# A searched order of all steps in place of planned dates, and other buffers for the last results

## The chip, the cores and the metric

One Trainium2 chip, one of its cores. The metric is the time of the whole program on that core in microseconds (us), median of several runs. One further execution was recorded by the hardware profiler; its rows are quoted below.

## The reference

Two stages. First, linear attention over 8 batches x 8 heads of 576 positions with 64 features:

```python
def phi(x):                                   # q and k: 8 x 8 x 576 x 64, w_phi: 64 x 128
    proj = np.einsum('bhsd,df->bhsf', x, w_phi)
    proj = proj - np.max(np.abs(proj), axis=-1, keepdims=True)
    return np.concatenate([np.exp(proj), np.exp(-proj)], axis=-1)
q_p, k_p = (phi(q), phi(k))
kv = np.einsum('bhsf,bhsd->bhfd', k_p, v)
z = np.sum(k_p, axis=2)
num = np.einsum('bhsf,bhfd->bhsd', q_p, kv)
den = np.einsum('bhsf,bhf->bhs', q_p, z)[..., None] + 1e-06
attn = num / den
```

Then a layer on the 4608 x 512 result x: `h = x @ w_in` (512 x 2048), `g = h * cos(h)`, `out = g @ w_out` (2048 x 512). All in float32.

## The kernel before

**Work.** A *unit* u is a pair of heads; there are 32. The 4608 rows of x are nine *chunks* c of 512 rows, and the inner width of 2048 is 16 blocks of 128 (ft). A *tile* is one chunk with one block; there are 144. Each becomes a float32 product out of three reduced ones (xh, xl, gh, gl and the two parts of w are high and low parts).

**Steps.** Each piece of work is a `Step` with an engine, a planned cost, the steps it depends on, and the buffers that it takes and uses. There are 2885 of them. A unit's steps on TensorE (PE) are q_mm (q projected, two steps), k_mm and k_end (k projected), k_sub (the row maximum subtracted, units 0 to 7), kv_mm, z_mm (the denominator) and n_mm (the numerator). ScalarE (ACT) copies q, computes the exponentials and copies kv; VectorE (DVE) takes maxima and divides; GpSimd (POOL) subtracts; SyncE (SP) issues all loads and stores. A tile's steps are mm1 (h, twelve matmuls, PE), copy and cosine and high (ACT), reduce, times and low (DVE), then mm2 (twelve matmuls into four banks, one for each 128 rows of the chunk). The first mm2 of a visit to a chunk is cut into four steps called `one`, one for each bank. When a visit ends, four `out_copy` steps (two on ACT, two on DVE) bring the banks into buffers o, and four `out_store` steps on SP send them off.

**Shapes of matmuls.** mm1, mm2, k_end and k_sub use the array as 128 x 128; q_mm and k_mm as two halves of 64 rows; kv_mm and n_mm as two halves of 64 columns; z_mm as four quarters of 32 columns.

**Order.** Chunks 0 to 2 are visited several times while the weights are converted; chunks 3 to 8 once each, with half of the weights loaded again per visit. Attention units stand between the tiles until all 32 are through. Which step comes when is decided in `plan()`: it keeps the time at which each engine, buffer and PSUM bank would be free by the planned costs, and takes of the steps that could start next the one with the earliest `due`. The dates come from a pace (`U_PE`, `T_PE`, `SPAN`, `SHIFT`, ...) and from two tables of corrections, `EARLIER` for each kind of step and `LATER` for each unit, block and visit. Each engine runs its steps in the order of the plan, and an instruction waits on the chip for the others by semaphores.

**Buffers.** Each name in `rings` has a fixed number of buffers, used in turn: o has 2, eq (exponentials of q) 3, gh and gl 3 each. There are 8 PSUM banks.

Of the kernel before, what the change touches and what calls it, by code (L numbers as in the profile page):

```python
# [17 lines left out]
P = 128  # L18
# [7 lines left out]
def phi_attention_then_cos_ffn(ctx: ExitStack, tc: tile.TileContext, qT, kT, vS, vT, w_phi, w_in, w_out, out):  # L26
# [36 lines left out]
    in_ring = {}  # L63
# [5 lines left out]
    class Step:  # L69
        def __init__(self, eng, cost, fn, deps=(), take=(), use=(), due=0.0, lat=None, table=None, port=False, kind=""):  # L70
# [4 lines left out]
            self.kind, self.due = kind, due + EARLIER.get(kind, 0.0)  # L75
# [3 lines left out]
            self.start, self.group = None, ""  # L79

            ring = tuple(b.ring for b in self.take if b.ring != "bank")
            self.after = [in_ring[ring]] if ring in in_ring else []
            if ring:
                in_ring[ring] = self
# [24 lines left out]
    LATER = {  # L109
# [7 lines left out]
    }  # L117
    TURN = dict(ACT=131.0, PE=97.0)
    SLACK = dict(PE=0.05, ACT=0.05, DVE=0.05, POOL=0.05, SP=0.05)
    LATENCY = dict(PE=0.35, ACT=0.25, DVE=0.2, POOL=0.25, SP=2.2)  # L120

    def plan():
        free = dict.fromkeys(LATENCY, 0.0)
        free["port"] = 0.0
        taken = {r: [] for r in rings}
        owner = [None] * 8
        todo = {e: [] for e in LATENCY}
        users = {}
        missing = {}
        for x in steps:  # L130
            missing[x] = len(x.deps) + len(x.after)
            for d in x.deps + x.after:
                users.setdefault(d, []).append(x)
        for x in steps:
            if not missing[x]:
                todo[x.eng].append(x)
        order = []
        table = dict(ACT=None, PE=None)

        def ready(x):  # L140
            t = max(free[x.eng], free["port"]) if x.port else free[x.eng]
            for d in x.deps:
                t = max(t, d.start + d.cost + d.lat)
            for b in x.take:
                if b.ring == "bank":
                    continue
                old = taken[b.ring]
                want = sum(1 for o in x.take[:x.take.index(b)] if o.ring == b.ring)
                k = len(old) + want - rings[b.ring]
                if k >= 0:  # L150
                    for v in old[k].users:
                        if v.start is None:
                            return None
                        t = max(t, v.start + v.cost + v.lat)
            n = sum(1 for b in x.take if b.ring == "bank")
            if n:
                open_ = [c[0] for c in empty()]
                if len(open_) < n:
                    return None
                t = max(t, open_[n - 1])  # L160
                if x.take[0].kind == "a" and x.due > FFN_DUE or x.take[-1].kind == "a" and x.due > FFN_DUE:
                    held = sorted(end_of(b) for b in owner if b is not None and b.kind == "a")
                    if len(held) + n > A_BANKS:
                        t = max(t, held[len(held) + n - A_BANKS - 1])
                        if t > 1e8:
                            return None
            return t

        def end_of(b):
            return max(1e9 if v.start is None else v.start + v.cost + v.lat for v in b.users)  # L170

        def empty():

            found = []
            for i, b in enumerate(owner):
                if b is None:
                    found.append((0.0, i))
                elif all(v.start is not None for v in b.users):
                    found.append((max(v.start + v.cost + v.lat for v in b.users), i))
            return sorted(found)  # L180

        while len(order) < len(steps):
            best = None
            for e, xs_ in todo.items():
                can = [(ready(x), x) for x in xs_]
                can = [c for c in can if c[0] is not None]
                if not can:
                    continue
                t = min(c[0] for c in can)
                x = min((c for c in can if c[0] <= t + SLACK[e]),  # L190
                        key=lambda c: c[1].due + (TURN[c[1].eng] if c[1].table not in (None, table.get(c[1].eng)) else 0.0))
                if best is None or x[0] < best[0]:
                    best = x
            assert best is not None, [(e, len(v)) for e, v in todo.items()]
            t, x = best
            x.start = t
            c = x.cost
            if x.table not in (None, table.get(x.eng)):
                c += SWITCH[x.table]
                table[x.eng] = x.table  # L200
                x.cost = c
            free[x.eng] = t + c
            if x.port:
                free["port"] = t + c
            spare = empty()
            for b in x.take:
                if b.ring == "bank":
                    b.slot = spare.pop(0)[1]
                    owner[b.slot] = b
                else:  # L210
                    taken[b.ring].append(b)
            todo[x.eng].remove(x)
            order.append(x)
            for y in users.get(x, []):
                missing[y] -= 1
                if not missing[y]:
                    todo[y.eng].append(y)
# [714 lines left out]
```

## Time and profile before

| | us |
|---|---|
| median of 3 runs | 1108.19 |
| range of the runs | 1107.01 to 1110.52 |
| the profiled execution's own time | 1109.67 |
| its span, first to last instruction | 1107.7 |
| TensorE busy | 1090.7 |
| VectorE busy | 743.3 |
| ScalarE busy | 724.2 |

The span is what the rows of the trace divide up; the execution's own time has 2.0 us more around it. An engine's busy time is a union over the span. Matmuls overlap in the profile, so the time of a matmul step is best read from its start to the start of the next one. The mean granted clock of TensorE over the span is 0.996 of full speed.

### The profile page before, as it was taken

How to read it: one execution, taken by the hardware profiler on the slowest of the kernel's cores; microseconds unless marked ns; L12 is line 12 of the kernel's file. 1: busy time of each engine (PE TensorE's matmuls, PEld its weight loads, DVE VectorE, ACT ScalarE, POOL GpSimd, SP SyncE). 2: the span in 40 equal slices, each digit the busy share in tenths (PEclk: the TensorE clock that was granted, in tenths of full speed). 3: DMA queues.
4: the chain of work that ended last, by engine and by line, in shares of the span. 5: the costliest groups of instructions: out<-in, count | busy, mean ns of one | idle time of the engine just before them, and what ended most of it. 6: DMA issues, size and time to landing. Idle time of an engine off the chain costs nothing.

```text
span 1107.7 us, 19579 instructions
## 1 busy us (share of the span) xinstructions
PE 1090.7 (98%) x7664; PEld 826.0 (75%) x7664; DVE 743.3 (67%) x1298; ACT 724.2 (65%) x1386; POOL 128.3 (12%) x91
## 2 busy tenths in 40 slices
PE   8999999999999999999999999999999999999998
PEld 5556566778887877778767787778676888888886
DVE  6889999988899775684587636784665334433432
ACT  6688889967775777664567746796577445444443
POOL 2655122000000210110031101120210000000000
PEclk9999999999999999999999999999999999999999
DMA  7466454556666433535243542444313611430531
GB/s 218 148 190 208 154 159 147 185 209 218 248 211 231 137 100 107 160 106 192 72 147 83 185 163 59 154 149 173 100 28 124 221 73 58 170 134 3 192 147 38
DMA packets 92604, 160.72 MB, mean 145 GB/s; under 512 B 43744, under 2 KB 52064, under 8 KB 84320
## 3 DMA queue, kind: packets, MB, share of 16 engines
q1 hardware_dynamic: 92512, 159.48, 42.8%
q8 instruction: 60, 0.98, 0.4%
q14 instruction: 32, 0.26, 0.1%
HBM read 117.51 MB, written 41.94 MB: 144 GB/s over the span
## 4 chain that ended last, share of the span: by engine, by line
PE 84%; DVE 5%; ACT 2%; DMA 0%; issue 0%; DVEq 0%
PE bank L783 34%; PE bank L817 12%; PE bank L818 11%; PE bank L819 11%; PE bank L676 4%; PE bank L627 4%; PE bank L439 2%; PE bank L666 2%; PE bank L477 2%; PE bank L633 1%; PE bank L552 0%; DMA sums<-o 0%; DVE o L862 0%; ACT L798 0%; DVE m_u__1175 L458 0%
## 5 line engine op out<-in xcount | busy, mean ns | idle before, releaser
L798 ACT ACT_TABLE_LOAD x22 | 28.2, 1283 | 0.4
L468 POOL TENSOR_TENSOR pq_u__3813<-pq_u__3813,bq_u__4068 128x576 f32<-128x576 f32 x2 | 3.6, 1802 | 173.8 <-DVE bq_u__4068 L464 173.8
L862 DVE COPY o<-bank 128x512 f32<-128x512 f32 x18 | 12.3, 683 | 8.3 <-PE bank L819 5.6
L860 ACT ACTIVATE o<-bank 128x512 f32<-128x512 f32 x18 | 10.7, 596 | 8.9 <-PE bank L819 5.7
L587 ACT ACT_TABLE_LOAD x11 | 14.1, 1283 | 3.6 <-PE bank L676 3.4
L856 DVE TENSOR_TENSOR o<-bank,o 128x512 f32<-128x512 f32 x24 | 15.9, 680 | 0.8 <-DMA o<-sums 0.8
L783 PE MATMUL bank<-xh_c__5067,w 128*128 128x512 f32 x32 | 13.1, 409 | 0.0
L582 ACT ACT_TABLE_LOAD x10 | 12.8, 1283 | 0.2
L783 PE MATMUL bank<-xh_c__6220,w 128*128 128x512 f32 x32 | 12.9, 403 | 0.0
L783 PE MATMUL bank<-xh_c__4501,w 128*128 128x512 f32 x32 | 12.8, 399 | 0.0
L783 PE MATMUL bank<-xh_c__7478,w 128*128 128x512 f32 x32 | 12.6, 392 | 0.0
L783 PE MATMUL bank<-xh_c__5730,w 128*128 128x512 f32 x32 | 12.5, 391 | 0.0
L783 PE MATMUL bank<-xh_c__5812,w 128*128 128x512 f32 x32 | 12.5, 391 | 0.0
L783 PE MATMUL bank<-xh_c__5957,w 128*128 128x512 f32 x32 | 12.5, 390 | 0.0
L783 PE MATMUL bank<-xh_c__6454,w 128*128 128x512 f32 x32 | 12.5, 390 | 0.0
L783 PE MATMUL bank<-xh_c__6586,w 128*128 128x512 f32 x32 | 12.5, 390 | 0.0
L783 PE MATMUL bank<-xh_c__4836,w 128*128 128x512 f32 x32 | 12.5, 390 | 0.0
L783 PE MATMUL bank<-xh_c__4504,w 128*128 128x512 f32 x32 | 12.5, 390 | 0.0
L783 PE MATMUL bank<-xh_c__4574,w 128*128 128x512 f32 x32 | 12.5, 390 | 0.0
L783 PE MATMUL bank<-xh_c__7145,w 128*128 128x512 f32 x32 | 12.5, 390 | 0.0
L783 PE MATMUL bank<-xh_c__7500,w 128*128 128x512 f32 x32 | 12.5, 390 | 0.0
L783 PE MATMUL bank<-xh_c__7882,w 128*128 128x512 f32 x32 | 12.5, 390 | 0.0
(3835 smaller groups left out, 4077.3 us busy)
## 6 DMA issues: line engine op xcount, KB each, us to landing
w<-w_parts SPq DMA_DIRECT2D x48, 1024.0 KB, 4.8
w_parts<-w SPq DMA_DIRECT2D x16, 1024.0 KB, 4.2
out<-o SPq DMA_DIRECT2D x36, 256.0 KB, 2.1
vmain<-vS SPq DMA_DIRECT2D x32, 256.0 KB, 3.7
sums<-o SPq DMA_DIRECT2D x24, 256.0 KB, 2.6
o<-sums SPq DMA_DIRECT2D x24, 256.0 KB, 3.0
vtail<-vT SPq DMA_DIRECT2D x64, 16.0 KB, 2.9
w_raw_f__130<-w_in SPq DMA_DIRECT2D x1, 512.0 KB, 5.7
```

The costliest lines, as they stand in the source:

```text
L439: PE.matmul(out=ps[j], lhsT=wphi[r, :], rhs=d["qr"][r, hf * HALF:(hf + 1) * HALF], start=True, stop=True)
L477: PE.matmul(out=ps[j][:, P * s:P * s + P], lhsT=x[r, P * s:P * s + P], rhs=wphi[r, :], start=(s == 0), stop=w, skip_group_check=True)
L587: ACT.activation(out=e[:, s, :], in_=d["pq"][:, j * S:(j + 1) * S], func=AF.Exp, scale=1.0 - 2.0 * s)
L627: PE.matmul(out=acc[c:c + 64, n, i, :], lhsT=e[:, s, P * n + c:P * n + c + 64], rhs=vmain[u % 2][:, s, i, :], start=(s == 0 and i == 0 and ...
L666: PE.matmul(out=ps[32 * g:32 * g + 32], lhsT=d["z"][:, 2 * n + j, :], rhs=d["eq", j][:, n, hf * HALF:(hf + 1) * HALF], start=(n == 0), sto ...
L676: PE.matmul(out=d["nps", hf][64 * j:64 * j + 64], lhsT=d["kv"][:, 2 * n + j, :], rhs=d["eq", j][:, n, cut[hf]], start=(n == 0 and hf == 0) ...
L783: PE.matmul(out=h, lhsT=a[:, cs], rhs=d[b, kt], start=(k == 0), stop=(k == 3 * KT - 1))
L798: ACT.activation(out=m["g"], in_=m["g"], func=AF.Sin, bias=halfpi, scale=1.0)
L817: PE.matmul(out=a, lhsT=gh[:, t], rhs=w[:, 0], start=first, stop=False)
L818: PE.matmul(out=a, lhsT=gh[:, t], rhs=w[:, 1], start=False, stop=False)
L819: PE.matmul(out=a, lhsT=gl[:, t], rhs=w[:, 0], start=False, stop=last)
L856: DVE.tensor_tensor(out=o, in0=bank(acc[tb]), in1=o, op=ALU.add)
```

## The change

`plan()` no longer chooses. A table `ORDER` names all steps, which are now 2888, in the order in which they are issued. `plan()` only walks through it, and still picks for each step the PSUM bank that is free first by the planned costs. Dates, both tables of corrections, the pace and the limits on banks are gone. In the last visit (chunk 8), the last tile's mm2 is also cut into four `one` steps, each out_copy depends on the step of its own bank, and the four results are written to buffers of eq in place of o.

```diff
-    EARLIER = {
-        "a.exp_k": 9, "a.exp_q": 21, "a.k_end": -134, "a.k_max": 107, "a.k_mm": -13, "a.k_sub": -347, "a.kv_mm": -14,
...
-    }
...
+    ORDER = [
+        0, 41, 2, 5, 3, 6, 7, 4, 8, 10, 11, 43, 46, 16, 57, 9, 12, 1192, 18, 20, 13, 44, 45, 48, 61, 19, 17, 58, 21,
...
+    ]
...
+        def end_of(v, eng):
+            return v.start + v.cost + (0.0 if v.eng == eng == "PE" else v.lat)
+
+        def empty(eng):
+
+            found = []
+            for i, b in enumerate(owner):
+                users = b.users if b is not None else []
+                if all(v.start is not None for v in users):
+                    found.append((max([0.0] + [end_of(v, eng) for v in users]), i))
+            return min(found)
+
+        for x in (steps[i] for i in ORDER):
             t = max(free[x.eng], free["port"]) if x.port else free[x.eng]
             for d in x.deps:
-                t = max(t, d.start + d.cost + d.lat)
+                t = max(t, end_of(d, x.eng))
             for b in x.take:
                 if b.ring == "bank":
+                    at, b.slot = empty(x.eng)
+                    owner[b.slot] = b
+                    t = max(t, at)
                     continue
...
-        return sorted(order, key=lambda x: x.start)
+        return [steps[i] for i in ORDER]
...
-            if first:
+            if first or last and v == len(course) - 1:
                 for tb in range(NB3):
                     def one(tb=tb, mm2=mm2):
                         mm2([tb])
 
-                    before = Step("PE", 0.68, one, [s7, before], take=[acc[tb]],
-                                  use=[gh, gl, slot], due=due_tile(n, 1.9), kind=stage + "one")
+                    before = Step("PE", 0.68, one, [s7, before], take=[acc[tb]] if first else [],
+                                  use=[gh, gl, slot] + ([] if first else [acc[tb]]), kind=stage + "one")
+                    done[tb] = before
...
-                o = d["o", tb] = new("o", [P, DM], F32, "o")
+                if v == len(course) - 1:
+                    o = d["o", tb] = new("eq", [P, 2, S], F32, "o_last")[:, 0, 0:DM]
+                else:
+                    o = d["o", tb] = new("o", [P, DM], F32, "o")
...
-            o = Buf("o")
+            o = Buf("o" if v < len(course) - 1 else "eq")
...
-            cp = Step(eng, 0.6 if eng == "ACT" else 0.68, out_copy, [before] + old, take=[] if old else [o],
-                      use=[acc[tb]] + ([o] if old else []), due=due_tile(nl, 2.5), kind=stage + "out_copy")
+            cp = Step(eng, 0.6 if eng == "ACT" else 0.68, out_copy, [done[tb] if v == len(course) - 1 else before] + old, take=[] if old else [o],
+                      use=[acc[tb]] + ([o] if old else []), kind=stage + "out_copy")
```

The order of instructions at three places. First TensorE around unit 17's kv_mm, at 454 to 474 us in the trace before; L783 is mm1, L627 kv_mm, L676 n_mm, L552 k_end, L439 q_mm, L477 k_mm, L666 z_mm (in the changed kernel L798, L642, L691, L568, L455, L493, L681). Shown is the first matmul of each step. Before:

```order
L783 MATMUL bank6_75<-xh0_c3__4501,w_2978 128x512
...
L627 MATMUL bank4_73<-vmain1_87,ek_u17__4725 64x65 x16
...
L676 MATMUL bank5_74<-eq_u16__4378,kv_u16__4709 64x64
...
L552 MATMUL bank3_72<-wphi_78,kr_u20__4823 128x128
L783 MATMUL bank2_71<-xh0_c3__4501,w_3075 128x512
...
L627 MATMUL bank6_75<-vmain0_86,ek_u18__4931 64x65 x16
...
L439 MATMUL bank5_74<-qr_u19__4428,wphi_78 128x288
...
L477 MATMUL bank3_72<-wphi_78,kr_u19__4429 128x128
...
L783 MATMUL bank2_71<-xh0_c3__4501,w_3226 128x512
...
L439 MATMUL bank6_75<-qr_u19__4428,wphi_78 128x288
...
L666 MATMUL bank5_74<-eq_u17__4779,z_u17__4974 32x288
```

And now:

```order
L798 MATMUL bank3_72<-xh0_c3__4458,w_2966 128x512
...
L642 MATMUL bank0_69<-vmain1_87,ek_u17__4812 64x65 x16
...
L681 MATMUL bank7_76<-eq_u16__4741,z_u16__4691 32x288
...
L691 MATMUL bank7_76<-eq_u16__4741,kv_u16__4690 64x64
...
L642 MATMUL bank3_72<-vmain0_86,ek_u18__4898 64x65 x16
...
L455 MATMUL bank1_70<-qr_u19__4588,wphi_78 128x288
...
L493 MATMUL bank7_76<-wphi_78,kr_u19__4589 128x128
...
L681 MATMUL bank3_72<-eq_u17__4809,z_u17__4984 32x288
...
L798 MATMUL bank0_69<-xh0_c3__4458,w_3249 128x512
```

The three mm1 that stood one by one between attention steps now stand ahead of them and behind them (two in front), z_mm and n_mm of one unit are neighbours, and k_end is elsewhere.

Second, TensorE at 42 to 51 us of the trace before, where k_mm of unit 5 (`kr_u5`) follows n_mm of unit 1; L633 is the end of kv_mm, L574 k_sub. Before:

```order
L633 MATMUL bank7_76<-vtail0_88,ek_u2__348 64x130 x4
L676 MATMUL bank5_74<-eq_u1__404,kv_u1__422 64x64
...
L477 MATMUL bank4_73<-wphi_78,kr_u5__514 128x128
...
L627 MATMUL bank3_72<-vmain1_87,ek_u3__518 64x65 x16
L574 MATMUL bank1_70<-mk_u4__580,minus_83 128x512
...
L666 MATMUL bank7_76<-eq_u2__605,z_u2__592 32x288
```

And now, with the same steps as L648, L691, L493, L642, L590, L681:

```order
L648 MATMUL bank3_72<-vtail0_88,ek_u2__313 64x130 x4
L691 MATMUL bank4_73<-eq_u1__361,kv_u1__435 64x64
...
L568 MATMUL bank0_69<-wphi_78,kr_u4__388 128x128
L590 MATMUL bank2_71<-mk_u4__577,minus_83 128x512
...
L642 MATMUL bank5_74<-vmain1_87,ek_u3__550 64x65 x16
...
L681 MATMUL bank7_76<-eq_u2__567,z_u2__571 32x288
...
L455 MATMUL bank3_72<-qr_u4__387,wphi_78 128x288
...
L493 MATMUL bank6_75<-wphi_78,kr_u5__611 128x128
```

The k_mm of unit 5 has moved behind k_sub of unit 4, kv_mm of unit 3 and z_mm of unit 2.

Third, the end of SP's queue, where the last weights are loaded and the last results stored. Before:

```order
L400 DMA w_10218<-w_parts14_112 128x2048
L400 DMA w_10255<-w_parts15_113 128x2048
L865 DMA out<-o_10461 128x512
L865 DMA out<-o_10463 128x512
L865 DMA out<-o_10467 128x512
L865 DMA out<-o_10470 128x512
```

And now:

```order
L417 DMA w_10266<-w_parts14_112 128x2048
L417 DMA w_10268<-w_parts15_113 128x2048
L884 DMA out<-o_last_10454 128x512
L884 DMA out<-o_10223 128x512
L884 DMA out<-o_last_10465 128x512
L884 DMA out<-o_last_10456 128x512
L884 DMA out<-o_last_10467 128x512
```

A store of the chunk before (o_10223) has moved behind the first of the last four, and the second and third of these have changed places.

## Rows read from the trace of the kernel before

**Rows 1.** The page: busy time of each engine; one kind of DMA.

```profile
PE 1090.7 (98%) x7664; PEld 826.0 (75%) x7664; DVE 743.3 (67%) x1298; ACT 724.2 (65%) x1386; POOL 128.3 (12%) x91
...
w<-w_parts SPq DMA_DIRECT2D x48, 1024.0 KB, 4.8
```

**Rows 2.** Windows: length, each engine's busy us, clock, DMA share, GB/s.

```profile
34.00:177.00 143.00, 137.32 (x1501) 86.27 (x1501) 131.89 (x263) 118.62 (x257) 54.70 (x31) 0.98 0.55 178
177.00:238.00 61.00, 60.95 (x522) 44.00 (x520) 55.46 (x95) 54.23 (x107) 5.59 (x4) 1.00 0.53 173
238.00:852.00 614.00, 614.00 (x4249) 470.92 (x4247) 431.75 (x748) 415.46 (x784) 53.94 (x34) 1.00 0.43 144
852.00:1100.00 248.00, 248.00 (x1094) 205.35 (x1095) 99.59 (x148) 113.47 (x190) 0.00 (x0) 1.00 0.32 116
```

**Rows 3.** The chain that ended last: start, us, what (two mm1).

```profile
365.02 2.72 PE bank L783 x12
...
469.77 2.94 PE bank L783 x12
```

**Rows 4.** Timeline of TensorE: start, us, line, tiles, shapes.

```profile
457.20 1.15 PE L627 MATMUL bank<-vmain,ek_u__4725 128*64 128x65 f32 x32
...
459.56 0.22 PE L676 MATMUL bank<-eq_u__4378,kv_u__4709 128*64 128x64 f32 x1
...
459.79 0.59 PE L676 MATMUL bank<-eq_u__4378,kv_u__4709 128*64 128x512 f32 x1
...
464.77 1.15 PE L627 MATMUL bank<-vmain,ek_u__4931 128*64 128x65 f32 x32
...
467.23 0.76 PE L439 MATMUL bank<-qr_u__4428,wphi 64*128 64x288 f32 x4
467.82 1.06 PE L477 MATMUL bank<-wphi,kr_u__4429 64*128 64x128 f32 x16
468.71 1.06 PE L477 MATMUL bank<-wphi,kr_u__4823 64*128 64x128 f32 x16
469.70 0.50 PE L783 MATMUL bank<-xh_c__4501,w 128*128 128x512 f32 x1
```

**Rows 5.** Waits of TensorE: waiting for whom, total us, times, longest.

```profile
PE bank L439 <- DMA qr_u__117<-qT: 5.2, 1, 5.2
PE bank L477 <- ACT ek_u__577 L582: 1.9, 1, 1.9
...
PE bank L439 <- DVE pk_u__1777 L569: 1.1, 1, 1.1
PE bank L627 <- ACT pq_u__1587 L446: 0.6, 1, 0.6
...
PE bank L676 <- DVE dn_u__1404 L682: 0.3, 1, 0.3
...
PE bank L574 <- DVE mk_u__923 L564: 0.2, 1, 0.2
```

**Rows 6.** Windows behind two of these waits (columns as in rows 2).

```profile
47.00:51.00 4.00, 4.00 (x47) 3.64 (x48) 3.85 (x11) 3.66 (x9) 0.00 (x0) 0.57 0.22 78
...
147.00:151.00 4.00, 4.00 (x32) 1.54 (x34) 3.13 (x8) 4.00 (x8) 0.00 (x0) 0.64 0.88 305
```

**Rows 7.** Timeline: first and last link of one tile's chain.

```profile
1064.47 0.60 ACT L789 ACTIVATE g_c__10238<-bank 128x512 int32<-128x512 f32 x1 [1.42 <-PE bank L783]
...
1068.52 0.69 DVE L54 TENSOR_TENSOR gl_c__10260<-g_c__10238,gh_c__10258 128x512 fp32r<-128x512 f32 x1 [0.76 <-ACT gh_c__10258 L49]
```

**Rows 8.** Timeline of the last 8 us: copies and the last matmul.

```profile
1100.45 0.60 ACT L860 ACTIVATE o<-bank 128x512 f32<-128x512 f32 x1 [4.76 <-PE bank L819]
...
1102.06 0.39 PE L819 MATMUL bank<-w,gl_c__10435 128*128 128x512 f32 x1
1103.20 0.60 ACT L860 ACTIVATE o<-bank 128x512 f32<-128x512 f32 x1 [2.16 <-DMA out<-o]
1103.99 0.69 DVE L862 COPY o<-bank 128x512 f32<-128x512 f32 x1 [2.17 <-DMA out<-o]
```

More of the change, by code (lines that the diff above doesn't have):

```diff
@@ L69, in phi_attention_then_cos_ffn, with __init__ @@
     class Step:
-        def __init__(self, eng, cost, fn, deps=(), take=(), use=(), due=0.0, lat=None, table=None, port=False, kind=""):
+        def __init__(self, eng, cost, fn, deps=(), take=(), use=(), lat=None, table=None, port=False, kind=""):
             self.eng, self.cost, self.fn, self.table = eng, cost, fn, table
@@ L78, in __init__ @@
                 self.table = SHAPE[kind[2:]]
[L79 to L84, printed above, removed]
+            self.start = None
             for b in self.take + self.use:
@@ L124, in plan @@
         free["port"] = 0.0
-        taken = {r: [] for r in rings}
+        table = {}
+        last = {}
         owner = [None] * 8
[L127 to L137, printed above, removed]
@@ L148, in ready @@
[L148 to L166, printed above, removed]
@@ L167, in ready @@
[L167 to L195, printed above, removed]
-            x.start = t
[L197 to L202, printed above, removed]
-            if x.port:
[L204 to L217, printed above, removed]
@@ L218, in plan @@
-        return sorted(order, key=lambda x: x.start)
+                held = last.setdefault(b.ring, [])
+                if len(held) >= rings[b.ring]:
+                    t = max([t] + [end_of(v, x.eng) for v in held[-rings[b.ring]].users])
+                held.append(b)
+            if x.table not in (None, table.get(x.eng)):
+                x.cost += SWITCH[x.table]
+                table[x.eng] = x.table
+            x.start = t
+            free[x.eng] = t + x.cost
+            if x.port:
+                free["port"] = t + x.cost
@@ L381, in convert @@
         raw, t = Buf("w_raw"), Buf("w_t")
[L382 to L389 removed]
+        s1 = Step("SP", 3.2, load, take=[raw], kind="w.load")
+        s2 = Step("ACT", 2.1, scale, [s1], take=[t], use=[raw], kind="w.scale")
+        s3 = Step("DVE", 2.55, bits, [s2], use=[t, raw], port=True, kind="w.bits")
+        s4 = Step("ACT", 1.05, high, [s3], take=[slot], use=[t], kind="w.high")
+        s5 = Step(name, cost, rest, [s3], use=[t], port=True, kind="w.rest")
+        s6 = Step(name, cost, low, [s4], use=[t, slot], port=True, kind="w.low")
+        s7 = Step(name, cost, add, [s5, s6], use=[t, slot], port=True, kind="w.add")
+        s8 = Step("SP", 3.2, store, [s7], use=[slot], kind="w.store")
         w_ready[ft] = [s7]
@@ L393, in phi_attention_then_cos_ffn, with reload @@
     w_slot = {}
-    def reload(ft, after, due):
+    def reload(ft, after):
         slot = w_slot[ft] = Buf("w")
@@ L400, in load @@
             SP.dma_start(out=w_tiles[ft].bitcast(F32), in_=w_parts[ft])
-        w_ready[ft] = [Step("SP", 3.2, load, w_stored[ft] + [after], take=[slot], due=due, kind="r.load")]
+        w_ready[ft] = [Step("SP", 3.2, load, w_stored[ft] + [after], take=[slot], kind="r.load")]
     stored, quotient, chain_v = {}, {}, {}
@@ L427, in load_v @@
                 SP.dma_start(out=vtail[u % 2][64 * j:64 * j + 64, j, 0:64], in_=vT[u][j])
-        ld = Step("SP", 1.9, load, take=[b["kr"], b["qr"]], due=due(-1.5), kind=phase + "load")
-        lv = Step("SP", 0.9, load_v, [chain_v.get(u - 1)], take=[b["v"]], due=due(-0.9), kind=phase + "load_v")
+        ld = Step("SP", 1.9, load, take=[b["kr"], b["qr"]], kind=phase + "load")
+        lv = Step("SP", 0.9, load_v, [chain_v.get(u - 1)], take=[b["v"]], kind=phase + "load_v")
         chain_v[u] = lv
@@ L593, in attention @@
             d["kb", i] = kb[i]
-        main = Step("PE", 0.88, lambda: k_mm(0), [ld], take=kb[:2] + pks[:2], use=[b["kr"]], due=due(0.12), kind=phase + "k_mm")
-        tail = Step("PE", 0.22, lambda: k_mm(1), [ld], take=[kb[2], pks[2]], use=[b["kr"]], due=due(0.12), kind=phase + "k_end")
+        main = Step("PE", 0.88, lambda: k_mm(0), [ld], take=kb[:2] + pks[:2], use=[b["kr"]], kind=phase + "k_mm")
+        tail = Step("PE", 0.22, lambda: k_mm(1), [ld], take=[kb[2], pks[2]], use=[b["kr"]], kind=phase + "k_end")
         for i in range(3):
@@ L607, in attention @@
             eks.append(Step("ACT", 1.06 if i < 2 else 0.42, lambda i=i: exp_k(i), [kms[i]] + gate, take=[e], use=[pks[i]] + ([kb[i]] if u in K_SUMS else []),
-                            due=due(0.35), table="e", kind=phase + "exp_k"))
+                            table="e", kind=phase + "exp_k"))
             ekb.append(e)
@@ L613, in attention @@
                             ([sm] if u in Q_SUMS else [qs[j]]) + gate, take=[e], use=[sb_[j], sb_[2]] if u in Q_SUMS else [b["pq"]],
-                            due=due(0.36), table="e", kind=phase + "exp_q"))
+                            table="e", kind=phase + "exp_q"))
             eqb.append(e)
@@ L651, in attention @@
                         take=[acc, b["kv"]] if first else [], use=[ekb[i] for i in p] + [b["v"]] + ([] if first else [acc, b["kv"]]),
-                        due=due(0.55), kind=phase + "kv_mm")
-        ko = Step("ACT", 0.6, kv_out, [last], use=[acc, b["kv"]], due=due(0.6), kind=phase + "kv_out")
+                        kind=phase + "kv_mm")
+        ko = Step("ACT", 0.6, kv_out, [last], use=[acc, b["kv"]], kind=phase + "kv_out")
         N0 = CT
@@ L749, in visit @@
             rawb.append(raw)
-            chain["x"] = [Step("SP", 0.9, load, [stored[NHP * bt + kt] for bt in batches] + chain["x"], take=[raw], due=due_tile(n0, -2), kind=stage + "load")]
+            chain["x"] = [Step("SP", 0.9, load, [stored[NHP * bt + kt] for bt in batches] + chain["x"], take=[raw], kind=stage + "load")]
             loads += chain["x"]
@@ L763, in visit @@
             x = Buf(f"x{kt}")
-            h = Step("ACT", 0.53, high, loads[kt] if v == 0 else [loads[kt]], take=[x], use=[rawb[kt]], due=due_tile(n0, -1), kind=stage + "x_high")
-            ks.append(Step("DVE", 0.68, low, [h], use=[x, rawb[kt]], due=due_tile(n0, -1), port=True, kind=stage + "x_low"))
+            h = Step("ACT", 0.53, high, loads[kt] if v == 0 else [loads[kt]], take=[x], use=[rawb[kt]], kind=stage + "x_high")
+            ks.append(Step("DVE", 0.68, low, [h], use=[x, rawb[kt]], port=True, kind=stage + "x_low"))
             xb.append(x)
         acc = [Buf("bank") for _ in range(NB3)]
+        done = {}
         before = None
@@ L843, in visit @@
             if c >= GROUP and i < N1:
-                reload(fts[N1 + i], before, due_tile(n, 2.0))
+                reload(fts[N1 + i], before)
         for tb in range(NB3):
```

135 lines of the change are left out of this document (30 added, 105 removed), and 156 rows, old and new, of tables (LATER, ORDER).

## The prediction

> **What bounds the kernel.** I read the page first. TensorE is busy 1090.7 of 1107.7 us; VectorE (67%) and ScalarE (65%) are far from that [rows 1]. Then I cut the span into stretches, to see where this holds [rows 2]: from 34 to 177 us TensorE is busy 137.32 of 143 us and VectorE 131.89 (92%), so the two wait for each other; from 238 to 852 us TensorE is busy 614.00 of 614 and VectorE 431.75 (70%); from 852 on the attention units are done and TensorE is again without a gap. The list of waits has 6.5 us on TensorE apart from its start, nine waits, all before 150 us [rows 5]. So after 238 us only TensorE's own work counts, and before it also who waits for whom.
>
> That own work has a part that no page shows as idle. The matmuls come in four shapes: the full array (mm1, mm2, k_end, k_sub), two row halves (q_mm, k_mm), two column halves (kv_mm, n_mm), four column quarters (z_mm). A mm1 of twelve matmuls takes 2.72 us in a run of its like, 2.94 us when it stands alone between a k_mm and a q_mm (the one at 469.77) [rows 3]. k_mm takes 0.89 us before another k_mm and 0.99 before a mm1 (467.82, 468.71, 469.70). A unit's kv_mm takes 2.36 us before n_mm, same shape (457.20 to 459.56), and 2.46 before q_mm (464.77 to 467.23) [rows 4]. Over all runs of one shape after 238 us, each compared in this way with its shortest form, a run of mm1 or mm2 costs 0.21 us beyond its matmuls (57 whole runs, 0.13 to 0.27), one of row halves 0.114 (37), one of column halves 0.113 (24); a run of z_mm is 1.107 us whatever follows (17), and one of k_end gives nothing measurable (17).
>
> [...]
>
> **The change, part by part.** *Instructions.* Both programs have the same ones on every engine, the 44 table loads on ScalarE included. Only order and banks differ, and four result tiles.
>
> *TensorE's order.* Counted in the order of both programs, the neighbours of different shape fall from 257 to 179. After the 15th unit's n_mm (238 us in the trace) the runs fall from 58 to 38 for mm1/mm2, 37 to 25 for row halves, 24 to 21 for column halves: 20 x 0.21 + 12 x 0.114 + 3 x 0.113 = 5.9 us. TensorE has no gap there, so all of it should come off. Ahead of that mark they fall from 22 to 13, 40 to 22 and 37 to 26: 9 x 0.21 + 18 x 0.114 + 11 x 0.113 = 5.2 us. There VectorE is 92% busy, and a TensorE that is done sooner may only wait. The ends are 0 (all of it becomes waiting) and 5.2. The nearest row is 177 to 238 us, where VectorE is 91% busy and TensorE still has 60.95 of 61 [rows 2]; against it stands 34 to 177 with 5.7 us of TensorE idle. I take half, 2.6 us.
>
> *Waits in the first 150 us.* The longest is u5's k_mm, which needs the bank that ScalarE's exponential of u3 reads: 1.9 us [rows 5]. [...] The new order breaks the old waits (that k_mm now stands behind k_end and k_sub of u4, a kv_mm of u3, z_mm of u2 and a q_mm of u4) and makes new ones that the trace does not hold. [...] I take 0, since the same engines are as full as before.
>
> *Covers after 238 us.* A tile's chain from ScalarE's first copy to gl takes 4.7 us (1064.47 to 1069.21) [rows 7]. In the old order at least three steps of 2.72 us stand between a mm1 and its mm2, 8.2 us; in the new one at least four, 10.9 us. Without that cover each mm2 would wait some 5 us; it grows, so I charge nothing. A reloaded weight lands in 4.8 us [rows 1]; between the mm2 that frees its buffer and the mm1 that reads it stand at least 10.9 us of matmuls in the old order and 8.2 in the new one, still more than it needs: 0, and some 4.8 us for each load if that cover were gone. z_mm and n_mm now stand side by side 17 times (2 before). Both write one bank that VectorE's reduction reads, and the old order has a wait of 0.3 us there [rows 5]. In 21 of the 32 units n_mm is now issued ahead of the reduction (10 before), so that VectorE waits for n_mm's first eight matmuls, 0.23 us from start to start (459.56 to 459.79) [rows 4], and TensorE does not wait. I cost it at 0; kv_mm and q_mm behind it would each be late by as much. Small new waits of attention steps are bounded below by 0 and above by a rival.
>
> *The end.* The last matmul starts at 1102.06; ScalarE's copy of the first bank starts at 1100.45, before the last tile is through [rows 8]. So copies wait for their own bank already, and cutting the last mm2 into four steps changes no wait: 0. The two buffers of o do cost: the third and fourth copy idle 2.16 and 2.17 us for a store's landing [rows 8]. With the three buffers of eq the third starts with its bank, and the fourth waits for the first store, which landed by 1103.20, instead of starting at 1103.99: 0.8 us earlier, and the end with it. On SP a store of the chunk before now stands between the first and the second of these; if it holds up the first landing by as much as the two old landings lie apart, 0.79 us, nothing is gained. I take 0.8, because it is issued behind the first.
>
> **Sum.** 5.9 + 2.6 + 0.8 = 9.3 us. The profiled execution took 1109.67 us (span 1107.7 and 2.0 around it), so 1100.4; the median of the three runs is 1.5 under it, so 1098.9, say 1099.
>
> **The rivals.** *A, the forecast:* 1099, own range 1095 to 1104, from 5.9 + 0 + 0 to 5.9 + 5.2 + 0.8 with 1 or 2 us of waits to either side. Chance 0.62.
>
> *B, the early waits go too.* [...] For it: the old waits hang on single neighbours, which a reordering breaks easily. Against it: VectorE has only 11.1 us free in 143. Chance 0.20.
>
> *C, no change: grouped attention steps wait.* Steps of one unit that stand closer together leave ScalarE less time between q_mm and what needs its copies. The old order has a wait of this kind, 0.6 us for kv_mm on the copy of q [rows 5]. One for each of the 17 units after 238 us is 10.2 us and cancels the 9.3: 1109; with ten of them it is 1105, where this measurement (some 0.3%, 3.3 us) no longer tells it from no change. Against it: ScalarE is 68% busy there, 415.46 of 614 us [rows 2]. Chance 0.12.
>
> *D, slower: new waits that drop the clock.* [...] Chance 0.06.
>
> **How the numbers follow.** The likeliest is A, 1099. 1090 to 1106 leaves out the lower part of B (0.08), the upper part of C (0.06) and D (0.06). Faster by over 0.3%: A, B and a quarter of C, 0.85; within 0.3%: most of the rest of C, 0.09; slower 0.06.
>
> **What would show it.** Right: TensorE without a gap from about 230 us to its end; mm1 alone at 2.94 us as rare as counted; TensorE's end some 8 us sooner, the last copy 1.5 us after the last matmul's end becoming 0.75; VectorE's busy time as before. Wrong: a wait list that is longer than 12 us on TensorE, clock below 1 in more than two places after the start, or gaps on TensorE behind ScalarE after 238 us (C); a first stretch shorter by over 8 us (B).

## The result and the profile after

The changed kernel takes 1094.07 us (median of 4 runs, 1093.87 to 1094.93), the kernel before 1108.58 beside it (4 runs, 1107.01 to 1110.52): a ratio of 0.987, 95% interval 0.985 to 0.989. The profiled execution took 1094.05 us, its span 1092.3 against 1107.7: 15.4 us less. In the profile of the changed kernel the lines are those after the arrow: L783 mm1 -> L798, L819 mm2 -> L834, L477 k_mm -> L493, L439 q_mm -> L455, L574 k_sub -> L590, L627 kv_mm -> L642, L676 n_mm -> L691. The experiments' tables are one line longer, so everything stands one line further there.

The page's first lines answer to [rows 1]; the windows to [rows 2] (columns as there, the last one shorter, since the program now ends sooner).

```profile
PE 1075.4 (98%) x7664; PEld 827.7 (76%) x7664; DVE 725.2 (66%) x1298; ACT 717.2 (66%) x1386; POOL 127.3 (12%) x91
```

```profile
34.00:177.00 143.00, 138.68 (x1591) 90.57 (x1589) 135.92 (x272) 122.10 (x270) 56.85 (x33) 1.00 0.55 169
177.00:238.00 61.00, 60.93 (x469) 45.10 (x468) 56.20 (x93) 51.27 (x93) 3.30 (x3) 1.00 0.41 129
238.00:852.00 614.00, 613.97 (x4267) 481.22 (x4266) 415.90 (x743) 412.55 (x786) 53.13 (x34) 1.00 0.46 153
852.00:1085.00 233.00, 233.00 (x1047) 191.17 (x1046) 94.22 (x148) 108.56 (x188) 0.00 (x0) 1.00 0.32 118
```

TensorE has the same 7664 matmuls, is as gapless after 238 us as it was, and has 15.3 us less to be busy. In its first stretch VectorE went up from 131.89 to 135.92 us: more of the program's start gets done there.

The list of waits of TensorE, which answers to [rows 5], and the windows that answer to [rows 6]:

```profile
PE bank L455 <- DMA qr_u__117<-qT: 5.3, 1, 5.3
PE bank L590 <- DVE mk_u__293 L580: 1.6, 1, 1.6
PE bank L590 <- DVE mk_u__850 L580: 1.3, 1, 1.3
PE bank L455 <- DMA qr_u__121<-qT: 1.1, 1, 1.1
PE bank L798 <- DVE pk_u__1058 L585: 0.8, 1, 0.8
PE bank L642 <- DVE pk_u__1306 L585: 0.6, 1, 0.6
```

```profile
47.00:51.00 4.00, 4.00 (x89) 3.06 (x87) 3.87 (x7) 3.02 (x8) 1.65 (x1) 1.00 0.47 129
147.00:151.00 4.00, 4.00 (x56) 3.08 (x52) 3.70 (x13) 3.11 (x11) 0.00 (x0) 1.00 0.46 141
```

With the five small ones left out here the waits behind the start come to 7.0 us (6.5 before): not fewer, but others, and both stretches of low clock are gone from this execution (0.57 and 0.64 before, 1.00 now). Of the four runs it alone has a mean clock of 1.000 over the span; the other three have 0.998.

The chain that ended last has both prices of mm1, as [rows 3] has: 2.72 us in company, 2.95 alone.

```profile
710.79 2.95 PE bank L798 x12
...
733.33 2.72 PE bank L798 x12
```

The timeline of the end answers to [rows 8]:

```profile
1087.22 0.60 ACT L879 ACTIVATE o_last<-bank 128x512 f32<-128x512 f32 x1 [0.76 <-PE bank L834]
...
1087.47 0.39 PE L834 MATMUL bank<-w,gl_c__10422 128*128 128x512 f32 x1
...
1088.63 0.69 DVE L881 COPY o_last<-bank 128x512 f32<-128x512 f32 x1 [1.40 <-DMA out<-o_last]
```

The third copy follows its bank, the fourth waits for a store and starts 0.77 us behind TensorE's last end (1.54 before). From TensorE's last end to the span's end it is 4.5 us, 5.2 before.

**Where the time went.** For each step on TensorE take the time from its first matmul to that of the next step, less the shortest such time of its kind in the trace before (0.218 us for k_end): its excess, which holds changes of shape, waits and lost clock alike. Summed over the stretches up to the n-th n_mm (us; the three kernels that change the end alone are within 0.3 us of the changed one and left out):

| | to 4th | 4th-8th | 8th-12th | 12th-15th | later | sum |
|---|---|---|---|---|---|---|
| before | 14.17 | 7.63 | 7.80 | 4.01 | 19.05 | 52.66 |
| after | 10.54 | 7.40 | 6.52 | 2.43 | 11.07 | 37.96 |
| x_old_order | 14.16 | 7.49 | 7.78 | 4.02 | 19.05 | 52.50 |
| x_early_new | 10.67 | 7.35 | 6.56 | 9.98 | 19.05 | 53.61 |
| x_early_new2 | 10.09 | 7.45 | 6.57 | 7.44 | 19.05 | 50.60 |
| x_early_old | 14.46 | 7.52 | 7.88 | 3.40 | 11.10 | 44.36 |
| x_split | 10.23 | 7.44 | 6.51 | 2.43 | 16.13 | 42.74 |
| x_dip | 12.99 | 7.68 | 6.72 | 4.02 | 19.05 | 50.46 |
| x_dip2 | 12.68 | 7.70 | 6.70 | 4.03 | 19.05 | 50.16 |
| y_search | 11.16 | 7.83 | 10.34 | 8.72 | 16.45 | 54.50 |
| y_written | 8.19 | 6.56 | 7.14 | 2.03 | 10.84 | 34.76 |

From before to after 8.0 us go late, 6.7 early, 0.8 at the end: 15.5 of the 15.4 by which the span is shorter (TensorE starts 0.1 later).

### The profile page after: what moved, and what is told of

It is laid out like the page before. It is cut to its first block, busy times and chain, and to the rows that moved or that the text cites. A ratio compares the mean times of both kernels' runs of the same rounds, so it can differ in the third digit from the quotient of the medians.

```text
span 1092.3 us, 19509 instructions
## 1 busy us (share of the span) xinstructions
PE 1075.4 (98%) x7664; PEld 827.7 (76%) x7664; DVE 725.2 (66%) x1298; ACT 717.2 (66%) x1386; POOL 127.3 (12%) x91
## 4 chain that ended last, share of the span: by engine, by line
PE 86%; DVE 6%; issue 0%; DMA 0%; ACT 0%; DVEq 0%
PE bank L798 35%; PE bank L832 12%; PE bank L833 12%; PE bank L834 12%; PE bank L691 4%; PE bank L642 4%; PE bank L681 2%; PE bank L455 2%; PE bank L493 2%; PE bank L648 1%; PE bank L568 0%; DVE g_c__1102 L809 0%; DMA out<-o_last 0%; DVE m_u__975 L466 0%; DVE g_c__1972 L809 0%
## 5 line engine op out<-in xcount | busy, mean ns | idle before, releaser
L798 PE MATMUL bank<-xh_c__7472,w 128*128 128x512 f32 x32 | 12.8, 400 | 0.0
L798 PE MATMUL bank<-xh_c__6688,w 128*128 128x512 f32 x32 | 12.8, 399 | 0.0
L798 PE MATMUL bank<-xh_c__5272,w 128*128 128x512 f32 x32 | 12.8, 399 | 0.0
L798 PE MATMUL bank<-xh_c__4458,w 128*128 128x512 f32 x32 | 12.7, 396 | 0.0
L798 PE MATMUL bank<-xh_c__7041,w 128*128 128x512 f32 x32 | 12.5, 390 | 0.0
L798 PE MATMUL bank<-xh_c__5868,w 128*128 128x512 f32 x32 | 12.5, 390 | 0.0
L798 PE MATMUL bank<-xh_c__8219,w 128*128 128x512 f32 x32 | 12.5, 390 | 0.0
L798 PE MATMUL bank<-xh_c__5790,w 128*128 128x512 f32 x32 | 12.5, 390 | 0.0
L798 PE MATMUL bank<-xh_c__7889,w 128*128 128x512 f32 x32 | 12.5, 390 | 0.0
L798 PE MATMUL bank<-xh_c__6645,w 128*128 128x512 f32 x32 | 12.5, 390 | 0.0
L798 PE MATMUL bank<-xh_c__5941,w 128*128 128x512 f32 x32 | 12.5, 390 | 0.0
L798 PE MATMUL bank<-xh_c__4514,w 128*128 128x512 f32 x32 | 12.5, 390 | 0.0
L798 PE MATMUL bank<-xh_c__4696,w 128*128 128x512 f32 x32 | 12.5, 390 | 0.0
L798 PE MATMUL bank<-xh_c__7074,w 128*128 128x512 f32 x32 | 12.5, 390 | 0.0
L798 PE MATMUL bank<-xh_c__8223,w 128*128 128x512 f32 x32 | 12.5, 390 | 0.0
```

Of the source, the lines that this page charges most:

```text
L798: PE.matmul(out=h, lhsT=a[:, cs], rhs=d[b, kt], start=(k == 0), stop=(k == 3 * KT - 1))
```

## Experiments

The theory: TensorE's changes of shape cost it time that nothing hides late and little hides early, and the old order's two waits cost low clock besides. The rivals: the new rule for banks, the four steps or the buffers did it; or waits alone did.

**Which part of the change, and where.** x_old_order has all of the change but the order; x_early_new, x_early_new2 and x_early_old join the two orders.

```diff
     ORDER = [
-        (the new order)
+        (the old one, with 2876 to 2879 for its last mm2;
+         or one order up to a step, then what the other has left)
     ]
```

> The changed kernel with the old order of steps in its table (banks still picked by its new rule, the last tile in four steps, the last results in eq buffers). Theory (the order is the gain, less the buffers at the end): the old time less the 0.8 us of the end, about 1107.8, TensorE's runs as before, both stretches of low clock back. Rival (the banks' rule, the four steps and the buffers are the gain): about 1094, as the changed kernel. Anything between divides the 14.5 us in that ratio.

Measured: 1109.23 us beside 1109.90, a ratio of 0.9997 (0.9988 to 1.0007). TensorE's excess is that of before in each stretch, and from TensorE's end (1102.76) to the span's (1107.2) it is 4.5 us as in the changed kernel. Banks and four steps do nothing that the trace shows, the buffers their 0.8 us at the end. The gain is the order's.

> The old order up to the 15th unit's n_mm, then what is left in the new order: 217 changes of shape, the late runs as in the changed kernel (38, 25, 21). Theory: 1094.1 plus the 6.7 us by which the two traces differ early, 1100.8, with the two stretches of low clock near 47 and 147 us back; by the prediction's early term of 2.6 us 1096.7. Rival (only the late order counts): 1094 to 1095.

Measured: 1100.32 us. The later excess is 11.10 (11.07 after), the early one that of before but for 0.6 us next to the joint (3.40 against 4.01). So the late order alone is worth the 8 us that the trace shows; what is missing to 1094.1 is 6.3, not the prediction's 2.6.

> The new order up to the 15th unit's n_mm, then what is left in the old order: 219 changes of shape, the late runs as before (58, 37, 24). Theory (late runs cost TensorE time that nothing hides): the changed kernel's 1094.1 plus 8.0 as the two traces differ there, 1102; by the prediction's 5.9 us 1100. Rival (waits and clock of the first stretch are the whole gain): 1094 to 1095.

Measured: 1108.68 us, and neither side had that. The list of waits, and windows from 200 us:

```profile
PE bank L643 <- ACT hs_c__2559 L806: 5.1, 1, 5.1
PE bank L591 <- DVE mk_u__293 L581: 2.1, 1, 2.1
```

```profile
200.00:204.00 4.00, 1.43 (x7) 0.85 (x5) 2.90 (x3) 4.00 (x10) 0.00 (x0) 1.00 0.74 217
204.00:208.00 4.00, 1.44 (x26) 1.45 (x28) 2.39 (x3) 3.92 (x11) 0.00 (x0) 0.55 0.37 144
208.00:212.00 4.00, 4.00 (x56) 3.53 (x53) 2.88 (x6) 3.90 (x8) 0.00 (x0) 0.60 0.47 197
```

At the joint a kv_mm waits 5.1 us for a bank that ScalarE has yet to read, and a low clock follows (0.55 and 0.60 over 4 us each): 7.5 us of excess in that one place (9.98 against 2.43). The stretches on either side of the joint are those of their own order to 0.15 us. One badly placed step undoes half of the gain.

> As x_early_new, but the two orders are joined earlier, behind the 12th unit's n_mm at some 170 us, where no step is left waiting for a bank at the joint; late runs as before (58, 37, 24). Theory: of the excess over the shortest forms 3.6 us go up to the 4th n_mm, 0.2 up to the 8th and 1.2 up to the 12th, as the traces of before and after differ there, and the old order's late part keeps its 19.05: 5.0 us under x_old_order, 1104. Rival (the first stretch's gain is lost again as waits when the late part is old): 1109, as x_early_new.

Measured: 1104.88 us, 4.4 under x_old_order. The table's row is from an execution of 1107.05 us, which is 2.2 over that median: up to the 12th n_mm it saves 5.3 us (24.11 against 29.43), and the next stretch, with a wait of 1.4 us behind the joint, gives 3.4 back (7.44 against 4.02). The mean clock of this execution is 0.998. Four of the seven runs have a mean clock of 0.999 or 1.000 and took 1103.8 to 1104.9 us, the other three 0.997 or 0.998 and 1107.0 to 1107.5. Early and late gains add up, less what the joint costs; neither needs the other.

**A price for changes of shape.** Thirteen late steps, each moved by one, such as a mm1 (1911) past a k_mm (704), ahead of a n_mm (612):

```diff
-        1911, 704, 612,
+        704, 1911, 612,
```

> The new order with 13 mm1 or mm2 behind 240 us each moved by one step, in between two attention steps: 13 more runs of mm1/mm2, 5 more of row halves, 2 more of column halves (199 changes of shape instead of 179), nothing else. Theory (a change of shape costs TensorE time): 13 x 0.21 + 5 x 0.114 + 2 x 0.113 = 3.5 us by the prediction's prices, so 1097.6, with no more waits on TensorE. Rival (waits are the gain, shapes cost nothing): 1094, within 0.5 us.

Measured: 1099.17 us, 5.1 more, all of it in the later stretch (16.13 against 11.07). The window has no gap:

```profile
238.00:852.00 614.00, 613.97 (x4248) 476.38 (x4247) 414.85 (x740) 409.95 (x781) 53.67 (x34) 1.00 0.45 151
```

So not waits, but for 0.5 us: one z_mm at 874 us takes that much longer (1.62 us against 1.11), and ScalarE's exponential of its second head runs until 874.91, in the middle of it. The rest by kind: 3.2 us for 13 runs of mm1/mm2 (0.25 each), 1.0 for five of row halves, 0.3 for two of column halves. A torn-up run costs more than the mean that the prediction used, 0.23 us over these 20 instead of 0.175.

**The low clock.** The old order with u5's k_mm (221) moved behind u3's second kv_mm (152); in x_dip2 behind u4's k_sub (183) too:

```diff
-        221, 109, 79, 80, 152, 223, 110, 81, 1321, 183,
+        109, 79, 80, 152, 221, 223, 110, 81, 1321, 183,
```

> The old order with one step moved: u5's k_mm stands behind u3's second kv_mm instead of ahead of it, so 1.08 us of matmuls now cover 1.08 of the 1.9 us that it waits for ScalarE. Theory (a wait drops the clock, and the low clock costs time of its own): wait 0.8 us, the low clock from 47.5 to 50.9 us gone or much shorter, up to 1.1 + 1.7 = 2.8 us under x_old_order, 1106.4. Rival 1 (only the wait counts): 1.1 us, 1108.1. Rival 2 (VectorE sets the pace there, the time comes back as other waits): 1109.

> As x_dip, with u5's k_mm behind the first k_sub of u4 too: 2.1 us of matmuls ahead of it. Theory: its wait is 0, no low clock near 47 us, and k_sub of u5 may wait some 1 us for its maximum, which is later now: 1.9 + 1.7 less 0 to 1.2, so 2.4 to 3.6 us under x_old_order, 1105.6 to 1106.8. Rival (VectorE sets the pace): 1109, with 2 us of new waits on k_sub.

Measured: 1106.48 and 1106.46 us, 2.8 under x_old_order (the kernel before took 1109.65 beside them, 1109.90 beside x_old_order). Waits of x_dip, windows of x_old_order, then of x_dip:

```profile
PE bank L494 <- ACT ek_u__577 L599: 1.3, 1, 1.3
PE bank L456 <- DVE pk_u__1777 L586: 1.1, 1, 1.1
```

```profile
47.00:51.00 4.00, 3.55 (x46) 3.24 (x46) 3.92 (x9) 3.98 (x10) 0.36 (x1) 0.61 0.23 76
147.00:151.00 4.00, 4.00 (x31) 1.60 (x32) 3.22 (x7) 3.89 (x8) 0.31 (x1) 0.59 0.86 296
```

```profile
47.00:51.00 4.00, 3.32 (x20) 1.85 (x20) 3.96 (x9) 3.98 (x11) 0.59 (x1) 1.00 0.27 78
147.00:151.00 4.00, 4.00 (x88) 2.86 (x84) 3.90 (x10) 4.00 (x7) 0.00 (x0) 1.00 0.97 370
```

The 1.7 us that the expectations put on the low clock near 47 us is an estimate from the trace of before: 0.43 of 4 us at a mean clock of 0.57 [rows 6]. The wait fell by only 0.5 us (1.86 to 1.34), yet 2.8 went, because the clock stays at 1.00 in both places. x_dip2 has no wait for the exponential, but 1.3 and 1.0 us on k_sub instead, and the clock is 1.00 there too, from 47 to 51 and from 146 to 152 us. All waits behind the start come to 6.4 us in x_old_order, 6.5 in x_dip and 7.6 in x_dip2, so the clock's part is all or nearly all of what both win. It holds beyond the profiled executions: the mean clock is 0.996 to 0.998 in all eleven runs of x_old_order, 0.999 or 1.000 in nine of ten of x_dip and in all eleven of x_dip2. The order at the second place was not touched at all (banks are picked anew behind the moved step): the q_mm that waits 1.13 us for VectorE does so in both kernels. The timeline of x_old_order, then that of x_dip:

```profile
145.61 1.57 PE L456 MATMUL bank<-qr_u__1550,wphi 64*128 64x288 f32 x6 [1.13 <-DVE pk_u__1777 L586]
```

```profile
144.27 1.48 PE L456 MATMUL bank<-qr_u__1550,wphi 64*128 64x288 f32 x6 [1.13 <-DVE pk_u__1777 L586]
```

Behind the first the clock is 0.59 from 147 to 151 us, behind the second 1.00. What makes the difference is not shown: no run here shifts the moment alone.

**The end.** x_tail gives the fourth result a buffer of o; y_store also moves the store of the chunk before (2725) ahead of the last tile's mm2, y_store_eq does only that.

```diff
-                if v == len(course) - 1:
+                if v == len(course) - 1 and tb < NB3 - 1:
                     o = d["o", tb] = new("eq", [P, 2, S], F32, "o_last")[:, 0, 0:DM]
...
-        2868, 2876, 2877, 2880, 2882, 2878, 2879, 2881, 2884, 2886, 2725, 2885, 2883, 2887,
+        2868, 2725, 2876, 2877, 2880, 2882, 2878, 2879, 2881, 2884, 2886, 2885, 2883, 2887,
```

> The changed kernel with the fourth of the last results in a buffer of o instead of the fourth turn of eq. Theory (the fourth copy waits only for the first store's landing): it starts with its bank at TensorE's end plus 0.1 instead of 0.77 behind it, and the end comes 0.7 us sooner: 1093.4, TensorE's end to the span's end 3.7 us instead of 4.43. Rival (the end hangs on the stores that queue ahead of it): no change, 1094.1.

> The changed kernel with the fourth of the last results in a buffer of o (as x_tail), and the store of the chunk before that stood behind the first of the last four now some 15 us earlier. Theory (at the end it is the transfers of five stores of 256 KB, without a gap from 1087.3 to 1091.0 us, that set the end, not the last copy): four stores instead of five, a fifth of 3.7 us, so the end 0.7 us sooner: TensorE's end to the span's end 3.7 us instead of 4.43, 1093.3. Rival (the end is a fixed delay behind the last copy or issue): as x_tail, 1093.7 to 1094.1.

> As y_store, but the fourth result stays in eq and its copy waits for the first store's landing, as in the changed kernel. Theory (transfers set the end): the first store lands sooner when nothing stands behind it, and the fourth's packets still find a busy queue: 0.3 to 0.7 us sooner, 1093.4 to 1093.8. Rival (the fourth copy sets the end once the old store is gone): 1094.1.

Measured: 1093.70, 1093.55 and 1093.89 us: at most 0.5 under the changed kernel, less than the runs of one kernel differ, and the spans are the same 1092.3. From TensorE's end to the span's end it is 4.4, 4.3 and 4.5 us, 4.5 in the changed kernel. In x_tail the fourth copy starts at 1087.98, at once, and nothing is gained. Windows of the changed kernel and of x_tail (last column GB/s):

```profile
1088.00:1089.00 1.00, 0.00 (x0) 0.00 (x0) 0.37 (x1) 0.00 (x0) 0.00 (x0) 1.00 1.02 379
1089.00:1090.00 1.00, 0.00 (x0) 0.00 (x0) 0.32 (x1) 0.00 (x0) 0.00 (x0) 1.00 1.02 383
```

```profile
1088.00:1089.00 1.00, 0.00 (x0) 0.00 (x0) 0.68 (x1) 0.00 (x0) 0.00 (x0) 1.00 1.02 377
1089.00:1090.00 1.00, 0.00 (x0) 0.00 (x0) 0.00 (x0) 0.00 (x0) 0.00 (x0) 1.00 1.02 385
```

The stores fill the DMA engines in both (a share of 1.02), whenever the last copy was. But y_store, with one store fewer, missed its 0.7 us too. The window of y_store shows a hole in the same place:

```profile
1088.00:1089.00 1.00, 0.01 (x1) 0.00 (x0) 0.69 (x1) 0.00 (x0) 0.00 (x0) 1.00 0.34 127
```

Its second store has been ready since its copy ended at 1087.38, but stands behind the third one in SP's queue (2885 ahead of 2883), whose copy ends at 1087.97. The last kernel below puts them in order.

**Another order.** y_search has another table, with the end of y_store and nearly the changed kernel's number of changes of shape.

> Another order of all steps: 181 changes of shape (179 in the changed kernel), after the 15th n_mm 36 runs of mm1/mm2 instead of 38, 25 of row halves and 21 of column halves as before, ahead of it 15, 27 and 24 instead of 13, 22 and 26; the end as in y_store. Theory (late runs have their price, early ones partly hide behind VectorE): 2 x 0.2 = 0.4 us late, within 1.5 us early to either side, 0.7 at the end: 1093, 1091.5 to 1094.5. Rival (order matters through waits alone): anything that its list of waits shows.

Measured: 1110.92 us, 18 us over the forecast and 0.15% slower than the kernel before (ratio 1.0015, 1.0005 to 1.0024). Its waits of TensorE, and the timeline at the longest (last matmul of z_mm, first of n_mm of one unit):

```profile
PE bank L692 <- DVE dn_u__2503 L698: 3.9, 1, 3.9
PE bank L692 <- DVE dn_u__999 L698: 3.6, 1, 3.6
PE bank L692 <- DVE dn_u__1680 L698: 3.5, 1, 3.5
PE bank L692 <- DVE dn_u__318 L698: 2.7, 1, 2.7
PE bank L692 <- DVE dn_u__5665 L698: 2.1, 1, 2.1
```

```profile
197.42 0.41 PE L682 MATMUL bank<-eq_u__2293,z_u__2402 128*32 128x288 f32 x1
201.76 0.37 PE L692 MATMUL bank<-eq_u__2431,kv_u__2401 128*64 128x64 f32 x1 [3.93 <-DVE dn_u__2503 L698]
```

n_mm stands right behind z_mm on TensorE and waits 3.93 us for VectorE's reduction. Its tail goes into the bank that the reduction reads. In this table `invert` is written ahead of n_mm in ten such units; in the changed kernel all seventeen neighbours have n_mm written first. y_written turns the ten round (n_mm 540 ahead of invert 537, and so on), and issues the last stores in the order of their copies:

```diff
-        598, 581, 537, 1414, 1408, 540,
+        598, 581, 540, 537, 1414, 1408,
...
-        2882, 2879, 2883, 2886, 2887, 2884, 2885,
+        2882, 2879, 2883, 2884, 2885, 2886, 2887,
```

> The order of y_search with one thing changed: in ten units where n_mm stands directly behind z_mm on TensorE, the step n_mm is written ahead of invert in the table instead of behind it (every engine keeps its own order of steps; banks are picked anew). At the end the last four stores are issued in the order of their copies. Theory (z_mm and n_mm write one bank, and whichever of n_mm and the reduction is written later waits for the other): the z_mm runs of y_search, 20.0 us over their shortest form against 1.25 us in the changed kernel, lose at least 15 us of that, as do the low clocks behind them: 1091 to 1095; and with the stores in order TensorE's end to the span's end is 3.8 us instead of 4.4. Rival (y_search is slow for the order of its steps itself, its neighbours or VectorE's load): 1108 to 1111.

Measured: 1090.02 us (ratio 0.9825, 0.9812 to 0.9839), 20.9 us under y_search and 4.1 under the changed kernel: the best of all here. The runs of z_mm fell from 20.0 to 0.2 us of excess, and from TensorE's end (1084.48) to the span's (1088.3) it is 3.8 us, 4.4 in y_search: 0.7 of the 20.9 us come from the order of the stores. Windows of y_search, then of y_written:

```profile
34.00:177.00 143.00, 133.97 (x1508) 87.51 (x1504) 128.40 (x265) 118.72 (x265) 53.31 (x31) 0.99 0.52 163
177.00:238.00 61.00, 57.07 (x490) 42.11 (x490) 52.25 (x86) 52.54 (x94) 5.61 (x4) 0.94 0.40 126
```

```profile
34.00:177.00 143.00, 138.01 (x1609) 91.19 (x1605) 135.00 (x275) 123.70 (x276) 56.46 (x33) 1.00 0.54 173
177.00:238.00 61.00, 61.00 (x454) 45.48 (x454) 55.58 (x89) 54.11 (x93) 2.81 (x2) 1.00 0.45 142
```

Each engine's steps stand in the same order in both, but for the last stores. Which of two instructions on different engines is written first, and so must be waited for, was worth more than the whole change. No run holds the banks fixed: `plan()` picks them anew, and 48 of its picks differ. But what went are the waits named above.

## Why the prediction came out as it did

The forecast was 1099.0 and its mechanism holds: the order is the gain (x_old_order), it comes from TensorE's own work, and nothing waits for it late. The measured 1094.07 is 4.9 us further down: inside the whole range, but 0.9 below A's own, on rival B's side of it. Two terms of the sum were too small, by 2.1 and 4.1 us. That 4.9 and not 6.2 is missing is luck: the forecast took 1.5 us off the profiled 1109.67 for the median of three runs, and 70 later runs of the kernel before have a median of 1109.8.

**Late, 5.9 us.** It measured 8.0 (x_early_old, and the table). The counts were right, the prices were not constant. By kind the excess fell from 12.10 to 7.39 for mm1/mm2 (4.7; counted 4.2), from 4.23 to 2.30 for row halves (1.93; 1.4), from 2.72 to 2.27 for column halves (0.45; 0.34), and by 0.89 for k_end, which was put at "nothing measurable". That was a mean of two: behind the 15th n_mm a k_end ahead of mm1 or mm2 took 0.05 us less than the 0.218 (11 times), one ahead of another shape 0.09 more (6 times); now fourteen stand ahead of mm1 or mm2, at 0.06 less, three ahead of another k_end, and none ahead of another shape. A price by the pair of neighbours would have caught it, a mean by run did not.

**Early, 2.6 us.** It measured 6.7, beyond the upper end of that term, because the term of 0 for the early waits should have been some 3.1: two stretches of low clock that did not come back, by the clock of 0.57 and 0.64 over 4 us each [rows 6] an estimate of 0.43 x 4 = 1.7 and 0.36 x 4 = 1.4 us. x_dip won 2.8 of that kind with one step moved. The rest, 3.6 us, is two thirds of the 5.2 that the counts gave; the prediction took half. VectorE had some room (131.89 to 135.92 us). That waits themselves would stay the same, 6.5 before and 7.0 after, was right; so rival B came in by half: the time at low clock went, the waits did not.

**The end, 0.8 us.** Right, also alone (x_old_order), and the copies came sooner, as the reason given has it. But the next bound was close behind: transfers and the order of the stores, not copies (x_tail, y_store, y_written).

**z_mm beside n_mm, 0.** Right for this order, and the likeliest to go wrong: the prediction named what decides it (which is issued ahead of which), and y_search shows the price of the other way, 18.8 us of z_mm's 20.0.

**Rivals C and D.** No gap after 238 us (613.97 of 614), so C fell. D's mechanism exists (x_early_new: 5.1 us of wait and 2.4 behind it), but this order has no such place in the profiled execution; and a wait has no fixed price here: behind the same 1.13 us the clock was 0.59 in x_old_order and 1.00 in x_dip.

**The signs.** TensorE's end came 14.6 us sooner instead of 8, the last copy starts 0.77 us behind it, as said. One sign failed: VectorE's busy time, expected as before, fell by 18.1 us (743.3 to 725.2) with the same 1298 instructions. Why is open. Most of the fall lies between 238 and 852 us (431.75 to 415.90), where TensorE has no gap in either kernel.

**Left open.** What decides whether a pause of 1 to 2 us drops the clock was not settled, but it is not the order alone. The kernel before ran 70 times beside the experiments, and the mean clock of each run was taken: 7 runs with 1.000 took 1106.6 to 1106.9 us, 23 with 0.998 took 1108.2 to 1110.1, 40 with 0.996 or less took 1109.5 to 1111.6. The profiled execution, with its two stretches, has 0.996; at 1.000 the same program is 3.6 us faster than at 0.996 or less (medians 1106.67 and 1110.24), close to the 3.1 estimated above for both. That the others had one or none of them is an estimate from these means. Against those 7 runs the changed kernel gains 12.6 us.

## What to carry to other kernels

Where one engine is busy without a gap, compare the same step's start-to-start time by its neighbours: here 0.1 to 0.25 us a change, some eighty times, is a per cent that no wait list shows. Before two steps that share a bank are put side by side, look which is written first: in y_search and y_written the later one waited for the earlier across engines (up to 3.9 us in y_search), with each engine's own order the same. A pause on TensorE can have a second price in the clock (0.61 over 4 us behind one of 1.9 us in x_old_order; x_dip, at 1.00, took 2.8 us less), so a short wait early in a program may be worth moving one step.

## What the runs showed of the hardware

A low clock can hide behind a lead. x_tail's profiled execution has one at 23 to 27 us that the changed kernel's does not, yet up to the 4th n_mm both have nearly the same excess (10.64 and 10.54), and the executions took 1094.07 and 1094.05 us. Windows of the changed kernel, then of x_tail:

```profile
23.00:27.00 4.00, 2.56 (x30) 1.29 (x32) 3.00 (x7) 3.18 (x9) 1.54 (x2) 1.00 0.79 247
```

```profile
23.00:27.00 4.00, 4.00 (x30) 1.70 (x32) 1.85 (x3) 1.23 (x6) 2.69 (x2) 0.57 0.36 80
```

That looks as if it cost nothing. The timeline shows where it went: the k_sub ahead of it and the q_mm behind it, in the changed kernel, then in x_tail.

```profile
24.44 0.49 PE L590 MATMUL bank<-mk_u__293,minus 128*128 128x128 f32 x2 [1.65 <-DVE mk_u__293 L580]
...
28.07 0.76 PE L455 MATMUL bank<-qr_u__251,wphi 64*128 64x288 f32 x4
```

```profile
22.94 0.52 PE L591 MATMUL bank<-mk_u__293,minus 128*128 128x128 f32 x2 [2.18 <-DVE mk_u__293 L581]
...
28.13 0.76 PE L456 MATMUL bank<-qr_u__251,wphi 64*128 64x288 f32 x4
```

x_tail came to the k_sub's wait 2.06 us ahead, for the most part since it lacks a wait of 1.10 us for a load that the changed kernel has at 8.67 us. It waits 0.53 longer, starts the k_sub 1.50 us sooner and the q_mm 0.06 us later: k_sub, z_mm and n_mm took 5.19 us instead of 3.63. So the low clock cost 1.56 us, all that was left of the lead.
